# Second layer: where the splits of the operands and one sum stand in the queues

## The chip, the cores and the metric

The kernel runs on one core of a Trainium2 chip. The metric is the time of the whole program on the device in microseconds (us). The engines are named as in the profile: PE (TensorE, matrix products), ACT (ScalarE), DVE (VectorE), POOL (GpSimd), SP (SyncE, which issues all DMAs here). Each works through its own queue in order; semaphores hold an instruction until what it needs is done.

## What is computed

Attention with a decay, then two feed-forward layers on 2304 tokens of width 512. The change lies in the second layer alone:

```python
def _moe2_ref(x, w_gate, w_val, w_out):
    g = x @ w_gate                          # 512 -> 1536
    silu = g * (1.0 / (1.0 + np.exp(-g)))
    val = x @ w_val
    return (silu * val @ w_out).astype(np.float32)   # 1536 -> 512
```

## The kernel before

**Seven products.** Both matrix multiplications of the second layer are done by blocks with seven products instead of eight. Sums and differences of blocks of the weights are made ahead and stored in DRAM; those of the activations are made on the fly. The order of the products is `PO = (1, 6, 2, 7, 5, 4, 3)`; the text calls them P0 to P6 in this order. The results come together in three PSUM tiles a, b and c: P0 goes to a and ACT copies it out as p (p1 in the code); P1 to b, and DVE drains u2 = b + p1; P2 is added to a, P3 to b, and DVE drains u3 = b + p1; P4 goes to c, P5 to b, P6 to c, each drained by DVE. A product that adds to a tile has to wait until the drain before it has read this tile: P2 for the copy of p, P3 for u2, P5 for u3.

**Splits.** Each operand of a product is fp32 cut into a high and a low part, and three partial products are summed. `split_c(i, src)` (L668) makes both: a cast on ACT (L672), then the difference by DVE, or by POOL for the products 2 and 5 (`LOWP`), shown as line L116. There is one buffer `c{i}` for each product, so the split for the next round can only run when the product has read the old one.

**Input half (`in2`, L769).** Two stages of weight columns, in each three passes over the tokens (768 tokens at a time), in each pass three groups q of seven products of 12 matmuls (L783). The four outputs of a group go through silu (L762: a sigmoid on ACT, two products on DVE for one block and on POOL for three) and are stored to DRAM as g. In the last group of a pass the splits for the next pass are made; `late` (L869) puts the split of P(k-1) behind Pk and, behind P6, also the split of P6 itself. In the middle group the four sums of x (`x_sums`, L680) for the next pass are made on DVE, one behind each of P0 to P3. SP reads the x of the pass after that (`x_read`) ahead of the first group.

**Output half (`out2`, L832).** Nine items of 128 columns of tokens (each of two row halves), `NIT = 9`. An item is seven products of 18 matmuls (L842) of the stored g (tiles `gt`, read by `g_load`) with weights that stay in SBUF. During item t the four sums of g for item t+1 are made (`g_sums`, L813, into the tiles `gs` and one `gt`), one behind each of P0 to P3: the first and the fourth on POOL, the second and the third on DVE (`SUMP = (0, 3)`); and the splits for item t+1 (`g_split`), by the same `late`. The sums and splits for item 0 are made in the last pass of the input half.

All instructions of the second layer keep, engine by engine, the order in which the code issues them (`in_order`, L539). So the place of a call in `after(i)`, which runs behind each product, is the place in the queues.

Of the kernel before, what the change touches and what calls it, by code (L numbers as in the profile page):

```python
# [9 lines left out]
F32 = mybir.dt.float32  # L10
# [38 lines left out]
NPASS, NQ, NST = 3, 6, 2  # L49
NIT = NPASS * CH // 128  # L50
TCL = 84
PO = (1, 6, 2, 7, 5, 4, 3)
LOWP = (2, 5)
SUMP = (0, 3)
POS_IN = {1: 0, 2: 1, 5: 2, 6: 3, 7: 4, 3: 5, 4: 6}
POS_OUT = {2: 0, 3: 1, 5: 2, 6: 3, 7: 4, 4: 5, 1: 6}
ORD1 = "0c152cw64cowwc"
# [41 lines left out]
def body(ctx: ExitStack, tc: tile.TileContext, qk, v, f, w_in, w_out, w_gate, w_val, w_out2, mask_c, ident_c, sel_c, out):  # L99
# [547 lines left out]
    free = []  # L647
    cp = [None]
    X, xid, cmb, wu = {}, {}, {}, {}
    jobs = []  # L650

    def slot_tile(shape, dtype, name):
        s = free.pop(0)
        t = wpools[0 if s < SA else 1].tile(shape, dtype, tag=f"w{s}", name=f"{name}{s}")
        return s, t
# [4 lines left out]
    def x_read(b, p):  # L660
        SP.dma_start(out=X[b], in_=x2[2 * p + b % 2][:, b // 2 * 2:b // 2 * 2 + 2])

    def u_read(u, i):
        s, t = slot_tile([128, 2, 2, 256], F32R, "wu")
        wu[u, i] = s, t
        SP.dma_start(out=t.bitcast(F32), in_=w_u[u][(POS_IN if u < NQ else POS_OUT)[i]])

    def split_c(i, src):  # L668
        n = src.shape[1]
        c = cp[0].tile([128, 2, 2 * CH], F32R, tag=f"c{i}", name=f"c{i}")  # L670
        c = cmb[i] = c.rearrange("p h (k t) -> p h k t", k=n)
        ACT.copy(out=c[:, 0], in_=src)  # L672
        subtract(POOL if i in LOWP else DVE, c[:, 1], src, c[:, 0])

    def tt(o, a, b, op, e=None):
        (e or DVE).tensor_tensor(out=o, in0=a, in1=b, op=op)  # L676
# [3 lines left out]
    def x_sums(e=None):  # L680
        return [lambda: tt(X[5], X[1], X[0], sub, e), lambda: tt(X[4], X[3], X[5], sub, e),
                lambda: tt(X[1], X[3], X[1], sub, e), lambda: tt(X[6], X[2], X[4], sub, e)]
# [79 lines left out]
    def silu(e, C, g, p, q, blk):  # L762
# [4 lines left out]
        SP.dma_start(out=g_d[p][blk, :, :, q], in_=g[:, blk].rearrange("p (m t) -> p m t", m=NPASS))  # L767

    def in2(p, q, after):  # L769

        at, bt = (ps.tile([128, 2, 512], F32, tag=t, name=t) for t in "ab")
        ct = ps.tile([128, 2, 512], F32, tag="c", name="c")
        a, b, c = (t[:, :, :CH] for t in (at, bt, ct))
        acc = {1: (a, 1, 0), 2: (a, 0, 1), 6: (b, 1, 0), 7: (b, 0, 0), 4: (b, 0, 1), 5: (c, 1, 0), 3: (c, 0, 1)}
        p1, u2, u3 = (wk.tile([128, 2, CH], F32, tag="u", name=n, bufs=6) for n in ("p1", "u2", "u3"))
        g = wk.tile([128, 4, CH], F32, tag="g", name="g", bufs=2)
        for i in PO:
            o, s, e = acc[i]
            for mem in range(2):
                n = 0  # L780
                for x, y in ((0, 0), (1, 0), (0, 1)):
                    for kt in range(2):
                        PE.matmul(o[:, mem], lhsT=wu[q, i][1][:, mem, x, 128 * kt:128 * kt + 128], rhs=cmb[i][:, y, kt],  # L783
                                  start=bool(s and n == 0), stop=(n == 5), skip_group_check=True)
                        n += 1
            if i == 1:
                ACT.copy(out=p1, in_=a)  # L787
            elif i == 6:
                tt(u2, b, p1, add)
            elif i == 2:  # L790
                silu(DVE, a, g, p, q, 0)
            elif i == 7:
                tt(u3, b, p1, add)
            elif i == 5:
                tt(u3, c, u3, add)
                silu(POOL, u3, g, p, q, 3)
            elif i == 4:
                tt(p1, b, p1, add)
                silu(POOL, p1, g, p, q, 2)
            else:  # L800
                tt(u2, c, u2, add)
                silu(POOL, u2, g, p, q, 1)
            after(i)

    GT = {}
    sums = {}

    def g_load(t):
        GT[t] = [slot_tile([128, NQ, 128], F32, "gt") for _ in range(4)]
        for e in range(4):  # L810
            SP.dma_start(out=GT[t][e][1], in_=g_d[t // NPASS][e, :, t % NPASS])

    def g_sums(t, k):  # L813
        g = [x[1] for x in GT[t]]
        s1, s2, s4 = (sums[e][1] for e in range(3))
        tt(*((s1, g[1], g[3], add), (g[1], g[0], g[1], sub), (s2, g[3], g[1], sub), (s4, g[2], s2, sub))[k], e=POOL if k in SUMP else DVE)

    def g_split(t, i):
        g = [x[1] for x in GT[t]]
        s1, s2, s4 = (sums[e][1] for e in range(3))  # L820
        split_c(i, {1: g[0], 6: s2, 2: g[2], 7: g[1], 5: s1, 4: g[3], 3: s4}[i])
        if i == 3:
            free.extend(x[0] for x in GT.pop(t))

    def rows(t, par):
        s0 = 128 * t
        for a, b in ((s0, min(s0 + 128, S)), (max(s0, S), s0 + 128)):
            if a < b:
                d = 2 * (a // S) + par
                yield a - s0, b - s0, d * S + a % S  # L830

    def out2(t, after):  # L832
        a, b, c = (ps.tile([128, 2, 512], F32, tag=n, name=n)[:, 0, :256] for n in "abc")
        acc = {1: (a, 1), 2: (a, 0), 6: (b, 1), 7: (b, 0), 4: (b, 0), 5: (c, 1), 3: (c, 0)}
# [30 lines left out]
    def fill(n=0):  # L865
        while jobs and len(free) > n:
            u_read(*jobs.pop(0))

    def late(fn, i):  # L869

        k = PO.index(i)
        if k:
            fn(PO[k - 1])
        if k == 6:
            fn(i)

    NQS = NQ // NST
    for st in range(NST):
        for p in range(NPASS):
            final = st == NST - 1 and p == NPASS - 1  # L880
            nxt = None if final else (p + 1) % NPASS
            for q in range(NQS * st, NQS * st + NQS):
                k = q - NQS * st

                def after(i):
                    if p == NPASS - 1:
                        free.append(wu.pop((q, i))[0])
                        fill()
                    if k == 1 and i in PO[:4]:
                        if final:  # L890
                            g_sums(0, PO.index(i))
                        else:
                            x_sums()[PO.index(i)]()
                    if k == NQS - 1:
                        late((lambda i: g_split(0, i)) if final else x_split, i)

                if k == 0 and not final:
                    for e in range(4):
                        x_read(e, nxt)
                in2(p, q, after)  # L900
                if k == 0 and p == 0 and st == 0:
                    jobs += [(u, i) for u in range(4, NQ) for i in PO]
            if st == NST - 1 and p == NPASS - 2:
                free.extend(xid.values())
                g_load(0)
                for e in range(3):
                    sums[e] = slot_tile([128, NQ, 128], F32, "gs")
                g_load(1)
                jobs += [(u, i) for i in PO for u in range(NQ, 9)]
                fill()  # L910
    fill()
    assert not jobs and len(free) == 4, (jobs, free)
    for t in range(NIT):
        if t + 2 < NIT:
            g_load(t + 2)

        def after(i):
            if t + 1 < NIT:
                if i in PO[:4]:
                    g_sums(t + 1, PO.index(i))  # L920
                late(lambda i: g_split(t + 1, i), i)

        out2(t, after)
    in_order(first)
# [57 lines left out]
```

## Time and profile before

| | |
|---|---|
| median of 3 runs (lowest, highest) | 1005.52 us (1004.41, 1006.17) |
| profiled execution, its own time | 1004.43 us |
| its span, first to last instruction | 1002.6 us |
| busy: PE, DVE, ACT, POOL | 982.5, 690.1, 505.6, 538.2 us |
| mean granted clock of PE | 0.994 |
| first matmul of the input half | 586.1 us |
| first matmul of the output half | 854.9 us |

PE is busy for 98% of the span; the other engines have room on average, but not in each stretch. The granted clock is given as a share of the full 2.4 GHz. Times in rows are counted from the first instruction of the span.

### The profile page before, as it was taken

Reading aid. Unit: us, or ns where it says so; the run is one execution under the profiler, and the core shown is the slowest. Engines: PE = TensorE matmul, PEld = TensorE weight load, DVE = VectorE, ACT = ScalarE, POOL = GpSimd, SP = SyncE. Lnnn points to the kernel's source line nnn. Section 1 sums busy time; section 2 is a strip of 40 time slices with the busy share of each in tenths; the row PEclk is TensorE's granted clock in tenths of the full one; section 3 lists DMA queues with packets and bytes.
Section 4 is the critical chain, followed back from the end, with each engine's and each line's share of the span. In section 5 each row is a group of like instructions: output and inputs, shape, how many; then the busy total and the mean of one; then the engine's idle time right before and its main releaser. Section 6 shows DMA issues by size and latency. Waiting matters only on the chain. (4 is left out here: it accounts for less than half of the span.)

```text
span 1002.6 us, 18483 instructions
## 1 busy us (share of the span) xinstructions
PE 982.5 (98%) x6728; PEld 938.5 (94%) x6728; DVE 690.1 (69%) x1302; ACT 505.6 (50%) x1112; POOL 538.2 (54%) x476
## 2 busy tenths in 40 slices
PE   8999999999999999999999999999999999899998
PEld 5787877899999999999999999999999999799998
DVE  5888887687788778777775546666666565566763
ACT  6888888355545555556555422332413232344431
POOL 3555654343248677687682014645645565846642
PEclk9999999999999999999999999999999999899999
DMA  5666564433457868778767772317732339643321
GB/s 198 191 184 216 185 205 151 141 102 124 160 178 232 250 216 269 242 224 260 231 206 256 253 270 63 111 51 265 262 117 69 107 120 404 242 158 133 121 106 42
DMA packets 108555, 183.36 MB, mean 183 GB/s; under 512 B 8720, under 2 KB 71984, under 8 KB 108464
## 3 DMA queue, kind: packets, MB, share of 16 engines
q1 hardware_dynamic: 108464, 182.18, 55.2%
q8 instruction: 53, 0.87, 0.4%
q14 instruction: 38, 0.31, 0.1%
HBM read 119.15 MB, written 63.00 MB: 182 GB/s over the span
## 5 line engine op out<-in xcount | busy, mean ns | idle before, releaser
L254 PE MATMUL h<-xh,w 128*128 128x384 f32 x768 | 149.5, 335 | 0.0
L613 PE MATMUL t<-gh,w 128*128 128x384 f32 x704 | 136.6, 335 | 1.8 <-ACT gh L598 1.8
L254 PEld LDWEIGHTS h<-xh,w 128*128 128x128 f32 x768 | 134.4, 188 | 0.5 <-issue 0.5
L613 PEld LDWEIGHTS t<-gh,w 128*128 128x128 f32 x704 | 123.1, 188 | 2.6 <-ACT gh L598 2.3
L783 PE MATMUL b<-c,wu 128*128 128x384 f32 x648 | 121.7, 335 | 3.5 <-DVE u L676 3.5
L590 ACT ACTIVATE n<-h 128x384 int32<-128x384 f32 x96 | 47.1, 491 | 143.7 <-PE h L254 132.4
L592 DVE SCALAR_TENSOR_TENSOR r<-h,n 128x384 f32<-128x384 f32 x96 | 53.4, 556 | 95.0 <-ACT n L590 94.6
L783 PEld LDWEIGHTS b<-c,wu 128*128 128x128 f32 x648 | 112.8, 188 | 5.2 <-DVE u L676 5.1
L765 POOL TENSOR_TENSOR s<-u,s 128x384 f32<-128x384 f32 x36 | 44.2, 1229 | 113.1 <-ACT s L764 101.5
L408 ACT ACTIVATE P<-P,mx 128x576 f32<-128x576 f32 (+4 forms) x160 | 87.5, 547 | 4.0 <-DVE mx L401 4.0
L676 DVE TENSOR_TENSOR u<-b,p 128x768 f32<-128x768 f32 (+1 forms) x54 | 41.8, 775 | 59.7 <-PE b L783 42.2
L254 PE MATMUL h<-xl,w 128*128 128x384 f32 x384 | 82.0, 334 | 0.0
L783 PE MATMUL a<-c,wu 128*128 128x384 f32 x432 | 81.4, 336 | 0.2
L783 PE MATMUL c<-c,wu 128*128 128x384 f32 x432 | 80.7, 334 | 0.0
L401 DVE CUSTOM_DVE_ANT_0 P<-s,mask 128x576 f32<-128x576 f32 (+4 forms) x160 | 68.1, 482 | 14.0 <-PE s L377 14.0
L783 PEld LDWEIGHTS a<-c,wu 128*128 128x128 f32 x432 | 75.2, 188 | 1.8 <-ACT p L787 1.8
L116 POOL TENSOR_TENSOR w<-ta,w 128x512 fp32r<-128x512 f32 x32 | 44.6, 1395 | 59.4 <-ACT w L191 32.0
L783 PEld LDWEIGHTS c<-c,wu 128*128 128x128 f32 x432 | 75.4, 188 | 0.0
L613 PE MATMUL t<-gl,w 128*128 128x384 f32 x352 | 75.2, 334 | 0.0
L842 PE MATMUL b<-wu,c 128*128 128x256 f32 x486 | 65.4, 290 | 5.0 <-DVE u L676 5.0
L764 ACT ACTIVATE s<-u 128x384 f32<-128x384 f32 x36 | 18.9, 524 | 98.8 <-DVE u L676 98.8
L254 PEld LDWEIGHTS h<-xl,w 128*128 128x128 f32 x384 | 67.9, 188 | 0.0
(116 smaller groups left out, 2198.8 us busy)
## 6 DMA issues: line engine op xcount, KB each, us to landing
wu<-wu SPq DMA_DIRECT2D x63, 512.0 KB
wraw<-in_w_out_dram SPq DMA_DIRECT2D x28, 512.0 KB
wu<-hi SPq DMA_DIRECT2D x54, 256.0 KB
gd<-g SPq DMA_DIRECT2D x72, 192.0 KB
gt<-gd SPq DMA_DIRECT2D x36, 384.0 KB
raw<-in_qk_dram SPq DMA_DIRECT2D x16, 576.0 KB
wu<-sums SPq DMA_DIRECT2D x36, 256.0 KB
xb<-x SPq DMA_DIRECT2D x24, 384.0 KB
```

The source lines that it names most:

```text
L116: eng.tensor_tensor(out=o, in0=a, in1=b.bitcast(F32), op=ALU.subtract)
L254: PE.matmul(ps, lhsT=w[:, a, 128 * kk:128 * kk + 128], rhs=b[:, kk], start=(n == 0), stop=(n == 3 * KD - 1))
L401: DVE.tensor_tensor_reduce(out=view(P[p][:rows, c0:c0 + ext], t), in0=ss[p % 2][:rows, SAT[t][0], SAT[t][1]], in1=view(mask[:rows, m1 - ex ...
L408: ACT.activation(out=o, in_=o, func=AF.Exp, scale=-1.0, bias=mxt[p % 8][:rows, t:t + 1], accum_out=smt[p // 2 % 3][:rows, p % 2, t:t + 1])
L590: ACT.activation(out=n, in_=h, func=AF.Copy, scale=INV2PI, bias=0.25)
L592: DVE.scalar_tensor_tensor(out=r, in0=h, scalar=INV2PI, in1=n, op0=ALU.mult, op1=ALU.subtract)
L613: PE.matmul(acc[m][:, :CH], lhsT=wo[:, q, 128 * m:128 * m + 128], rhs=x, start=(j == a and n == 0), stop=False)
L676: (e or DVE).tensor_tensor(out=o, in0=a, in1=b, op=op)
L764: ACT.activation(out=s, in_=C[:, 0], func=AF.Sigmoid)
L765: e.tensor_tensor(out=s, in0=C[:, 0], in1=s, op=ALU.mult)
L783: PE.matmul(o[:, mem], lhsT=wu[q, i][1][:, mem, x, 128 * kt:128 * kt + 128], rhs=cmb[i][:, y, kt], start=bool(s and n == 0), stop=(n == 5) ...
L842: PE.matmul(ot, lhsT=cmb[i][:, x, q], rhs=wu[NQ + q // 2, i][1][:, q % 2, y], start=bool(s and n == 0), stop=(n == 3 * NQ - 1), skip_group ...
```

## The change

`late` becomes a queue of one entry that lives on across groups and items: behind a product it issues the split that waits in it and takes up the split of the product just issued. So the split of P6 is now issued behind P0 of the next group or item; the other six stay where they were. The sums of x and of g move one product further on, and the first sum of g goes from POOL to DVE (`SUMP = (3,)`). For the items, the sums 0 and 1 stand behind P1, sum 2 behind P2, sum 3 behind P3. The reads of x, the first reads of g and the reads of g two items ahead are issued behind P1 of the next group or item instead of ahead of its P0.

```diff
-SUMP = (0, 3)
+SUMP = (3,)
...
-    def late(fn, i):
-
-        k = PO.index(i)
-        if k:
-            fn(PO[k - 1])
-        if k == 6:
-            fn(i)
+    pend = []
+
+    def late(fn=None, i=None):
+
+        if pend:
+            f, k = pend.pop(0)
+            f(k)
+        if fn:
+            pend.append((fn, i))
...
-                    if k == 1 and i in PO[:4]:
+                    if final and k == 0 and i == PO[1]:
+                        free.extend(xid.values())
+                        g_load(0)
+                        for e in range(3):
+                            sums[e] = slot_tile([128, NQ, 128], F32, "gs")
+                        g_load(1)
+                        jobs.extend((u, i) for i in PO for u in range(NQ, 9))
+                        fill()
+                    if k == 1 and i in PO[1:5]:
                         if final:
-                            g_sums(0, PO.index(i))
+                            g_sums(0, PO.index(i) - 1)
                         else:
-                            x_sums()[PO.index(i)]()
+                            x_sums()[PO.index(i) - 1]()
                     if k == NQS - 1:
                         late((lambda i: g_split(0, i)) if final else x_split, i)
-
-                if k == 0 and not final:
-                    for e in range(4):
-                        x_read(e, nxt)
+                    else:
+                        late()
+
+                    if k == 0 and not final and i == PO[1]:
+                        for e in range(4):
+                            x_read(e, nxt)
+
...
     for t in range(NIT):
-        if t + 2 < NIT:
-            g_load(t + 2)
 
         def after(i):
+            k = PO.index(i)
             if t + 1 < NIT:
-                if i in PO[:4]:
-                    g_sums(t + 1, PO.index(i))
-                late(lambda i: g_split(t + 1, i), i)
+                for n in ((), (0, 1), (2,), (3,), (), (), ())[k]:
+                    g_sums(t + 1, n)
+                late(lambda i, t=t: g_split(t + 1, i), i)
+            else:
+                late()
+            if k == 1 and t + 2 < NIT:
+                g_load(t + 2)
```

The queue of ACT at the end of the first pass, before. The casts to `c_7792` and `c_7795` are the splits of P5 and P6 for the next pass, `p_7805` is the copy of P0 of the next pass:

```order
L764 ACTIVATE s<-u_7664 128x384
L672 CAST c_7792<-xb_6943 128x768
L672 CAST c_7795<-xb_6864 128x768
L787 COPY p_7805<-a 128x768
L764 ACTIVATE s<-a 128x384
```

The same place now:

```order
L764 ACTIVATE s<-u_7664 128x384
L672 CAST c_7792<-xb_6943 128x768
L787 COPY p_7798<-a 128x768
L672 CAST c_7815<-xb_6864 128x768
L764 ACTIVATE s<-a 128x384
```

The copy and the cast for P6 have changed places.

The queue of DVE at the same place, before (`u_7806` is the drain u2 of the next pass's first group):

```order
L676 TENSOR_TENSOR u_7664<-c,u_7664 128x768
L116 TENSOR_TENSOR c_7792<-xb_6943,c_7792 128x768
L116 TENSOR_TENSOR c_7795<-xb_6864,c_7795 128x768
L676 TENSOR_TENSOR u_7806<-b,p_7805 128x768
L765 TENSOR_TENSOR s<-a,s 128x384
```

And now:

```order
L676 TENSOR_TENSOR u_7664<-c,u_7664 128x768
L116 TENSOR_TENSOR c_7792<-xb_6943,c_7792 128x768
L116 TENSOR_TENSOR c_7815<-xb_6864,c_7815 128x768
L676 TENSOR_TENSOR u_7799<-b,p_7798 128x768
L765 TENSOR_TENSOR s<-a,s 128x384
```

The order of DVE is the same there: the subtraction for P6 stands ahead of u2 in both.

The queue of DVE in item 1 of the output half, before, from its drain u2 (`u_9976`) to its drain u3 (`u_9977`); `gt` and `gs` are the sums for item 2, L116 the splits for it:

```order
L116 TENSOR_TENSOR c_9961<-gs_9362,c_9961 128x768
L676 TENSOR_TENSOR u_9976<-b,p_9975 128x256
L676 TENSOR_TENSOR gt_9790<-gt_9789,gt_9790 128x768
L116 TENSOR_TENSOR c_10019<-gt_9789,c_10019 128x768
L676 TENSOR_TENSOR gs_9361<-gt_9792,gt_9790 128x768
L116 TENSOR_TENSOR c_10042<-gs_9361,c_10042 128x768
L676 TENSOR_TENSOR u_9977<-b,p_9975 128x256
```

And now (u2 is `u_9965`, u3 `u_9966`):

```order
L116 TENSOR_TENSOR c_9987<-gs_9395,c_9987 128x768
L676 TENSOR_TENSOR u_9965<-b,p_9964 128x256
L676 TENSOR_TENSOR gs_9393<-gt_9840,gt_9842 128x768
L676 TENSOR_TENSOR gt_9840<-gt_9839,gt_9840 128x768
L116 TENSOR_TENSOR c_10011<-gt_9839,c_10011 128x768
L676 TENSOR_TENSOR gs_9394<-gt_9842,gt_9840 128x768
L116 TENSOR_TENSOR c_10042<-gs_9394,c_10042 128x768
L676 TENSOR_TENSOR u_9966<-b,p_9964 128x256
```

The first sum (`gs_9393`), on POOL before, stands between u2 and the second sum.

## Rows read from the trace of the kernel before

**Rows 1.** Waits of PE over the span: waiter <- awaited: us in total, times, longest

```profile
PE b L842 <- DVE u L676: 5.0, 2, 4.7
PE b L783 <- DVE u L676: 3.5, 5, 0.7
```

**Rows 2.** Timeline, first pass boundary: start us, us, engine, line, operation [idle before <-releaser]

```profile
629.86 2.24 PE L783 MATMUL a<-c,wu 128*128 128x384 f32 x12
...
631.94 2.24 PE L783 MATMUL b<-c,wu 128*128 128x384 f32 x12
...
632.78 3.60 DVE L116 TENSOR_TENSOR c<-xb,c 128x768 fp32r<-128x768 f32 x2 [1.66 <-ACT c L672]
633.01 2.55 POOL L116 TENSOR_TENSOR c<-xb,c 128x768 fp32r<-128x768 f32 x1
633.39 0.79 ACT L787 COPY p<-a 128x768 f32<-128x768 f32 x1
...
634.23 2.38 PE L783 MATMUL a<-c,wu 128*128 128x384 f32 x12
...
636.30 0.94 DVE L676 TENSOR_TENSOR u<-b,p 128x768 f32<-128x768 f32 x1
...
637.30 2.38 PE L783 MATMUL b<-c,wu 128*128 128x384 f32 x12 [0.69 <-DVE u L676]
```

**Rows 3.** Timeline, item 0 of the output half

```profile
860.56 1.72 POOL L765 TENSOR_TENSOR s<-u,s 128x384 f32<-128x384 f32 x1
861.34 0.41 DVE L676 TENSOR_TENSOR u<-b,p 128x256 f32<-128x256 f32 x1
...
862.36 1.01 POOL L766 TENSOR_TENSOR g<-u,s 128x384 f32<-128x384 f32 x1
863.33 1.84 POOL L676 TENSOR_TENSOR gs<-gt,gt 128x768 f32<-128x768 f32 x1
...
864.06 2.32 PE L842 MATMUL c<-wu,c 128*128 128x256 f32 x18
...
865.20 0.96 DVE L676 TENSOR_TENSOR gt<-gt,gt 128x768 f32<-128x768 f32 x1 [3.45 <-POOL gs L676]
...
871.03 4.21 PE L842 MATMUL b<-wu,c 128*128 128x256 f32 x18 [4.65 <-DVE u L676]
```

**Rows 4.** Stretch 868 to 870: us, busy PE PEld DVE ACT POOL, PEclk, DMA

```profile
868.00:870.00 2.00, 0.00 (x0) 0.00 (x0) 1.15 (x1) 2.00 (x3) 1.97 (x2) 0.59 0.96 315
```

**Rows 5.** Timeline, item 2 of the output half, and P5 of item 7

```profile
892.01 1.85 POOL L676 TENSOR_TENSOR gs<-gt,gt 128x768 f32<-128x768 f32 x1
...
894.86 0.37 ACT L846 COPY p<-a 128x256 f32<-128x256 f32 x1 [1.26 <-PE a L842]
...
897.09 0.42 DVE L676 TENSOR_TENSOR u<-b,p 128x256 f32<-128x256 f32 x1 [1.55 <-PE b L842]
897.43 0.95 DVE L676 TENSOR_TENSOR gt<-gt,gt 128x768 f32<-128x768 f32 x1
898.30 0.95 DVE L116 TENSOR_TENSOR c<-gt,c 128x768 fp32r<-128x768 f32 x1
...
900.21 0.83 ACT L672 CAST c<-gs 128x768 fp32r<-128x768 f32 x1 [0.66 <-DVE gs L676]
900.25 1.86 POOL L676 TENSOR_TENSOR gs<-gt,gs 128x768 f32<-128x768 f32 x1 [6.40 <-ACT g L850]
...
901.08 1.86 DVE L116 TENSOR_TENSOR c<-gs,c 128x768 fp32r<-128x768 f32 x1 [0.95 <-ACT c L672]
901.14 2.32 PE L842 MATMUL c<-wu,c 128*128 128x256 f32 x18
...
902.86 0.41 DVE L676 TENSOR_TENSOR u<-b,p 128x256 f32<-128x256 f32 x1
...
903.32 2.42 PE L842 MATMUL b<-wu,c 128*128 128x256 f32 x18
...
979.48 2.42 PE L842 MATMUL b<-wu,c 128*128 128x256 f32 x18
```

More of the change, by code (lines that the diff above doesn't have):

```diff
@@ L902, in body @@
                     jobs += [(u, i) for u in range(4, NQ) for i in PO]
[L903 to L910, printed above, removed]
     fill()
-    assert not jobs and len(free) == 4, (jobs, free)
+    assert not jobs
     for t in range(NIT):
-        if t + 2 < NIT:
-            g_load(t + 2)
         def after(i):
+            k = PO.index(i)
             if t + 1 < NIT:
-                if i in PO[:4]:
-                    g_sums(t + 1, PO.index(i))
-                late(lambda i: g_split(t + 1, i), i)
+                for n in ((), (0, 1), (2,), (3,), (), (), ())[k]:
[5 more added lines that the diff above has]
+                g_load(t + 2)
         out2(t, after)
```

## The prediction

> **What bounds the kernel now.** I read the page's busy shares first: the matrix engine (PE) is busy 98% of 1002.6 us, so a change that touches no matmul can only win back what PE stands still or runs slowly in the second layer. The list of waits gives that: PE waits there for VectorE (DVE) alone, 5.0 us in two places of the output half and 3.5 us in five places of the input half [rows 1]. Then I read the stretches around these places in order of time.
>
> Products are called P0 to P6 in the order of issue (1, 6, 2, 7, 5, 4, 3); "split k" is the cast on ACT and the subtraction that make the operand of Pk for the next pass or item. P3 may not start before the drain u2 = b + p1 has read PSUM tile b after P1, and P5 not before the drain u3 has read it after P3. Both drains are on DVE, behind whatever stands ahead of them in its queue.
>
> At a pass boundary [rows 2] products follow each other by 2.08 us (629.86 to 631.94). P2 is due at 634.02 and starts at 634.23, after ACT's copy of p; P3 is due at 636.10 and starts at 637.30, 0.06 us after u2 has ended (636.30 + 0.94). So 1.20 us are lost, five times. DVE came late to u2 because two subtractions took 3.60 us from 632.78 on: POOL's own subtraction ran from 633.01 to 635.56, and the second one on DVE ended only 0.82 us after that.
>
> In the output half the largest stop is in item 0 [rows 3]: P4 starts at 864.06, takes 2.32 and ends at 866.38; P5 starts at 871.03. DVE spent this time on the sums for item 1, and the second of them (865.20) had to wait for the first, which is POOL's (863.33 + 1.84 = 865.17); POOL was late because it still had silu to do. In this stop the granted clock fell: 0.59 on average from 868 to 870 us [rows 4], which with levels 1 and 0.5 (2.4 and 1.2 GHz) puts the fall at 868.36, 2.0 us after PE had stopped. P5 then took 4.21 us [rows 3] where the same product takes 2.42 in item 2 [rows 5]: 1.79 us more.
>
> Item 2 stands for items 1 to 7 [rows 5]. P5 starts at 903.32, 2.18 us after P4 (901.14), and from item 2 to item 7 it comes every 15.23 us (903.32 to 979.48, five items), 2.18 for each of seven products: PE runs evenly, P5 is not held. But u3 ends at 902.86 + 0.41 = 903.27, 0.05 us ahead of it. DVE's queue from u2 to u3 fills the time between P1 and P5 with nothing to spare.
>
> **The change, part by part.** *Split 6 one product later, at five pass boundaries.* On ACT the copy of p now stands ahead of the last cast; it can start where the cast did, one cast (0.83, [rows 5]) earlier, so P2 is no longer held: 0.21 us. But on DVE the last subtraction still stands ahead of u2, since it is issued after P0 and u2 after P1. Its cast now ends about 0.8 us later, near 634.3, while the subtraction could not start before POOL's had ended at 635.56. So u2 ends at 637.24 as before, P3 starts at 637.30, and what P2 wins P3 waits. I take 0 for the five boundaries. Bounds: 0.2 us less each if the earlier copy helps after all, 0.2 us more each if the later cast does hold the subtraction; 1.0 us either way. The reads of x move behind P1 of the next group, but in SP's queue they stand behind the same stores as before, so they cost nothing; the sums of x stand one product later behind u2 instead of ahead of it, in a group where PE waits for nothing. Without that cover a sum ahead of u3 would cost what it takes, 0.95.
>
> *The first sum of the next item's activations, from POOL to DVE.* It stands between u2 and the second sum. Neighbours there start 0.87 us apart (897.43 to 898.30, [rows 5]), and POOL is idle until the third sum is done, so the new one takes 0.87 us and pushes everything behind it: the third sum, the cast that waits for it (900.21), POOL's fourth sum (900.25), the subtraction beside it (901.08, 1.86 long) and u3. P5 then starts at 903.32 + 0.87 and is that much late in items 1 to 7: 7 x 0.87 = 6.09 us. On POOL nothing on the path is won: its sum ran at 892.01 for 1.85 us, to 893.86, and DVE came to the second sum only at 897.43. Bounds: 0 if the queue turns out to have room that these rows hide, 7 x 0.95 = 6.7 if the sum costs its whole duration.
>
> *Split 6 across items.* Its cast now follows the copy of p (894.86 + 0.37 = 895.23) and takes 0.83, the subtraction 0.95: it ends near 897.05, and u2 starts at 897.09. It just fits; if it did not, u2 and so P5 would come up to 0.2 us later in each item (1.4 us in all). I take 0. The loads two items ahead keep their place in SP's queue, behind the stores of the item before.
>
> *Item 0* [rows 3]. u2 starts at 861.34 as before. The first sum comes up on DVE 0.34 us later (as the second does now, [rows 5]), while POOL has silu from 860.56 to 862.28 and the second half of it from 862.36. Where the two engines met, one waited for the other: the silu at 860.56 took 1.72 and the one at 862.36, with DVE idle, 1.01. So I let them take turns: first sum to 862.28 + 0.83 = 863.11, POOL's second half to 863.96, second sum to 864.79. From the end of the second sum to P5 it is 903.32 - 898.38 = 4.94 us in item 2. P5 at 869.73 instead of 871.03: 1.30 us won. Bounds: 2.6 if the sums meet no silu (863.50 + 4.94 = 868.44), 1.0 if the first sum waits for both halves (863.37 + 0.83 + 0.87 + 4.94 = 870.01). The stop is still 869.73 - 866.38 = 3.35 us, longer than the 2.0 after which the clock fell, so I leave the 1.79 us where they are; bounds: all of it won, or as much again lost if the clock comes back later.
>
> *The sums of item 0 itself,* in the last pass: POOL's one (1.85) now stands between two silu steps and delays two stores of g and the weight loads behind them in SP's queue by up to 2 us. POOL's next work after them comes later than that, and the products that need these weights come over 10 us later. 0.
>
> *Sum:* 0 + 6.09 - 1.30 = 4.79 us. The profiled execution took 1004.43 us (1002.6 and 1.8 around it), so 1009.22; it lies 1.09 below the median of the runs (1005.52). On the median's scale: 1005.52 + 4.79 = 1010.3 us.
>
> **The rivals.** *The forecast (0.60):* VectorE's queue in the output half becomes the bound: 1010.3; with the low bound of item 0 and of the boundaries 6.09 - 2.6 - 1.0 = 2.5, so 1008.0, with the high ones 6.7 - 1.0 + 1.0 = 6.7, so 1012.2.
>
> *The clock holds in item 0 (0.12).* The stop shrinks from 4.65 to 3.35 us; if the clock stays up, 1.79 us are won: 1008.5. For it speaks the shorter stop and that after the short stops at the pass boundaries P3 ran at full speed (2.38 us, [rows 2]); against it that the fall came after 2.0 us.
>
> *The boundaries are cured (0.10).* If u2 no longer waits behind the last subtraction there, 5 x 1.20 = 6.0 us go: 1004.3. For it: the last split does leave the tail of the pass. Against it: DVE's order, in which that subtraction still stands ahead of u2.
>
> *The sum leaves the slow engine and the path gets shorter (0.13), faster than before.* The subtraction at 901.08 takes 1.86 beside POOL and 0.95 alone (the length of the one at 898.30). If POOL, with one sum less, takes its fourth sum and its own subtraction at times that leave this one free, the queue loses 0.91 and gains 0.87: nothing is lost in items 1 to 7, item 0 wins 1.30 + 0.91, and its stop of about 2.4 us may spare the clock: 1005.5 - 0.3 - 2.2 - 1.8 = 1001.2. It decides from the point where POOL's fourth sum does not start with the end of the third; the rows show it starting 0.04 us beside the cast (900.21 and 900.25), so I hold it unlikely. The Trainium skill (GPSIMD Engine Reference, 4.1 Engine selection) says to put elementwise work on VectorE, as GpSimd needs about twice the time for operations with two inputs. The trace agrees (1.85 against 0.95), and by that rule alone eight moved sums would win 8 x 0.9 = 7.2 us; it leaves out which of the two queues PE waits for.
>
> *More than the sum is late (0.05):* if the moved split also holds u2, or the clock falls in some of the seven new stops of about 0.9 us, 1.8 us each: 1013 and above.
>
> **How the numbers follow.** A measurement of this kernel can tell about 0.2%, 2.0 us, from no change. Slower by more: the forecast but for its edge, most of the clock's case and the last one, 0.70. Within: the cured boundaries, the rest of the clock's case and that edge, 0.15. Faster: the shorter path and a part of the cured boundaries, 0.15. The likeliest case's own range is 1008.0 to 1012.2; to leave out no more than 2 in 10 it has to reach down to the cured boundaries: 1004.2 to 1012.2.
>
> **What would show it.** In the profile after: PE's waits for u in the output half nine times instead of two, each of items 1 to 7 with about 0.9 us before P5, and an item every 16.1 us; on DVE two sums back to back behind u2; in item 0 P5 about 1.3 us earlier against its P3, with a clock below 1; at the pass boundaries P2 on time and P3 late by 1.2 us as before. The prediction is wrong if items still come every 15.2 us, or if PE's wait for u is gone from the input half.

## The result, and the profile after

| | before | changed |
|---|---|---|
| median | 1006.01 us (6 runs) | 1011.13 us (6 runs) |
| ratio to before | | 1.0054, 95% interval 1.0039 to 1.0069 |
| profiled execution, its own time | 1004.43 us | 1011.03 us |
| span | 1002.6 us | 1009.2 us |

The change makes the kernel 0.54% slower, 5.1 us by the medians, where 4.8 were forecast (1010.3 us). The two profiled executions differ by 6.6 us. Of these, 1.8 lie ahead of the second layer, where no instruction has moved: its first matmul starts at 586.1 us before and at 587.9 now. From there to the end it is 416.5 and 421.3 us, 4.8 more. The starts of the matmuls in the timelines divide this further:

| us | before | changed |
|---|---|---|
| input half, first matmul to first matmul of item 0 | 268.77 | 268.90 |
| item 0, P0 to P0 of item 1 | 22.38 | 20.70 |
| items 1 to 7, each | 15.24 | 16.15 |

The waits of PE for the drains u (waiter <- awaited: us in total, times, longest), against [rows 1]:

```profile
PE b L842 <- DVE u L676: 9.0, 9, 3.3
PE b L783 <- DVE u L676: 5.3, 5, 1.1
```

In the output half there are nine waits instead of two, as forecast; the longest is shorter (3.3 against 4.7). In the input half there are five as before, and longer.

The first pass boundary, against [rows 2] (start us, us, engine, line, operation, idle before):

```profile
633.71 2.24 PE L783 MATMUL b<-c,wu 128*128 128x384 f32 x12
...
634.42 0.79 ACT L787 COPY p<-a 128x768 f32<-128x768 f32 x1
...
634.79 2.57 POOL L116 TENSOR_TENSOR c<-xb,c 128x768 fp32r<-128x768 f32 x1
635.11 0.83 ACT L672 CAST c<-xb 128x768 fp32r<-128x768 f32 x1
...
635.79 2.25 PE L783 MATMUL a<-c,wu 128*128 128x384 f32 x12
635.98 2.20 DVE L116 TENSOR_TENSOR c<-xb,c 128x768 fp32r<-128x768 f32 x1 [0.33 <-ACT c L672]
...
638.10 0.94 DVE L676 TENSOR_TENSOR u<-b,p 128x768 f32<-128x768 f32 x1
...
639.10 2.35 PE L783 MATMUL b<-c,wu 128*128 128x384 f32 x12 [1.06 <-DVE u L676]
```

P2 (635.79) now follows P1 (633.71, 2.08 earlier) on time, since the copy of p stands ahead of the last cast. But the second subtraction on DVE, whose cast ends at 635.94, starts at 635.98 and, beside POOL's (634.79 to 637.36), takes 2.20 us, so it ends 0.82 us after POOL's, as it did before; u2 follows it at 638.10, and P3 starts at 639.10, 5.39 us after P1. Before, it started 5.36 us after P1.

Item 0, against [rows 3]:

```profile
862.48 1.72 POOL L765 TENSOR_TENSOR s<-u,s 128x384 f32<-128x384 f32 x1
863.26 0.41 DVE L676 TENSOR_TENSOR u<-b,p 128x256 f32<-128x256 f32 x1
...
863.60 1.42 DVE L676 TENSOR_TENSOR gs<-gt,gt 128x768 f32<-128x768 f32 x1
...
864.28 1.61 POOL L766 TENSOR_TENSOR g<-u,s 128x384 f32<-128x384 f32 x1
865.05 1.66 DVE L676 TENSOR_TENSOR gt<-gt,gt 128x768 f32<-128x768 f32 x1
...
865.98 2.32 PE L842 MATMUL c<-wu,c 128*128 128x256 f32 x18
...
871.12 0.41 DVE L676 TENSOR_TENSOR u<-b,p 128x256 f32<-128x256 f32 x1
...
871.59 3.34 PE L842 MATMUL b<-wu,c 128*128 128x256 f32 x18 [3.29 <-DVE u L676]
...
877.49 2.32 PE L842 MATMUL a<-wu,c 128*128 128x256 f32 x18
```

The two sums follow u2 on DVE, each beside half of POOL's silu (1.42 and 1.66 us instead of 0.95). P5 starts 5.61 us after P4; it was 6.97.

The granted clock there, against [rows 4] (busy times of PE, PEld, DVE, ACT, POOL, then PEclk, DMA share, GB/s):

```profile
870.00:871.50 1.50, 0.00 (x0) 0.00 (x0) 1.50 (x2) 1.50 (x3) 1.50 (x2) 1.00 1.00 371
871.50:873.00 1.50, 1.41 (x10) 1.41 (x11) 1.41 (x3) 0.07 (x1) 1.50 (x2) 0.90 0.99 385
873.00:875.00 2.00, 2.00 (x12) 2.00 (x11) 0.74 (x2) 0.00 (x0) 2.00 (x1) 0.50 0.43 171
875.00:877.00 2.00, 2.00 (x14) 2.00 (x14) 0.39 (x1) 0.83 (x1) 0.39 (x1) 0.72 0.35 131
```

It is still full while PE stands (868.30 to 871.59), and falls about 1.1 us after PE has started again: with levels 1 and 0.5, a mean of 0.90 over 871.5 to 873 puts the fall at 872.7. By 877 it is back. From P5 to P0 of item 1 (871.59 to 877.49) it is 5.90 us; in item 2 (905.37 to 909.78, next rows) it is 4.41.

Item 2, against [rows 5]:

```profile
893.64 2.32 PE L842 MATMUL a<-wu,c 128*128 128x256 f32 x18
...
895.80 2.32 PE L842 MATMUL b<-wu,c 128*128 128x256 f32 x18
...
898.16 0.42 DVE L676 TENSOR_TENSOR u<-b,p 128x256 f32<-128x256 f32 x1
898.50 0.95 DVE L676 TENSOR_TENSOR gs<-gt,gt 128x768 f32<-128x768 f32 x1
899.48 0.96 DVE L676 TENSOR_TENSOR gt<-gt,gt 128x768 f32<-128x768 f32 x1
...
900.36 0.95 DVE L116 TENSOR_TENSOR c<-gt,c 128x768 fp32r<-128x768 f32 x1
...
902.28 2.32 PE L842 MATMUL c<-wu,c 128*128 128x256 f32 x18
902.31 1.85 POOL L676 TENSOR_TENSOR gs<-gt,gs 128x768 f32<-128x768 f32 x1 [9.26 <-issue]
...
903.14 1.85 DVE L116 TENSOR_TENSOR c<-gs,c 128x768 fp32r<-128x768 f32 x1 [0.96 <-ACT c L672]
...
904.91 0.41 DVE L676 TENSOR_TENSOR u<-b,p 128x256 f32<-128x256 f32 x1
...
905.37 2.41 PE L842 MATMUL b<-wu,c 128*128 128x256 f32 x18 [0.78 <-DVE u L676]
...
909.78 2.32 PE L842 MATMUL a<-wu,c 128*128 128x256 f32 x18
```

Two sums now stand between u2 (898.16) and the split at 900.36. From u2 to u3 it is 6.75 us, before 5.77: 0.98 more. P5 starts 3.09 us after P4, before 2.18, and the item takes 16.14 us from P0 to P0 (893.64 to 909.78).

### The profile page after: what moved, and what is told of

Same layout as the page of the kernel before. It is cut to its first block, busy times and chain, and to the rows that moved or that the text cites. A ratio compares the mean times of both kernels' runs of the same rounds, so it can differ in the third digit from the quotient of the medians.

```text
span 1009.2 us, 18462 instructions
## 1 busy us (share of the span) xinstructions
PE 982.4 (97%) x6728; PEld 939.2 (93%) x6728; DVE 694.0 (69%) x1311; ACT 505.0 (50%) x1112; POOL 518.2 (51%) x467
## 5 line engine op out<-in xcount | busy, mean ns | idle before, releaser
L765 POOL TENSOR_TENSOR s<-u,s 128x384 f32<-128x384 f32 x36 | 40.8, 1134 | 123.7 <-ACT s L764 122.1
L116 POOL TENSOR_TENSOR w<-ta,w 128x512 fp32r<-128x512 f32 x32 | 44.9, 1403 | 60.0 <-ACT w L191 32.8
L842 PEld LDWEIGHTS b<-wu,c 128*128 128x128 f32 x486 | 60.9, 194 | 10.8 <-DVE u L676 10.8
```

The costliest lines, as they stand in the source:

```text
L116: eng.tensor_tensor(out=o, in0=a, in1=b.bitcast(F32), op=ALU.subtract)
L765: e.tensor_tensor(out=s, in0=C[:, 0], in1=s, op=ALU.mult)
L842: PE.matmul(ot, lhsT=cmb[i][:, x, q], rhs=wu[NQ + q // 2, i][1][:, q % 2, y], start=bool(s and n == 0), stop=(n == 3 * NQ - 1), skip_group ...
```

## The experiments

Every kernel was timed beside the kernel before on the same chip; the ratios are to it, with their 95% intervals in brackets. Times of single steps are from the one profiled execution of each run. "Behind Pk" is the place in the queues where an operation is issued.

**1. The first sum on DVE in its old place.** Edit of the kernel before:

```diff
-SUMP = (0, 3)
+SUMP = (3,)
```

> The kernel before with one edit: the first sum of g on DVE instead of POOL, in its old place behind P0, so on DVE ahead of u2. Theory (what costs is the place between u2 and u3): DVE is idle there for about 1.5 us in items 1 to 7, so items keep 15.2 us; in item 0 P5 comes about 1.3 us earlier, with a longer wait at P3 (about 2.2 us instead of 0.5) and a shorter one at P5. 1003.0 to 1005.5 us. Rival 1 (DVE has too much work wherever the sum stands): items 16.1 us, about 1011. Rival 2 (the moved splits cost, not the sum): 1004.5, as the theory, so this run tells theory and rival 1 apart.

Measured: 1003.48 us, ratio 0.9977 (0.9963 to 0.9992). Items 2 to 7 take 15.24 us, item 1 15.53, item 0 19.23 (22.38 before). DVE's rows in an item:

```profile
892.57 0.95 DVE L676 TENSOR_TENSOR gs<-gt,gt 128x768 f32<-128x768 f32 x1
...
894.89 0.42 DVE L676 TENSOR_TENSOR u<-b,p 128x256 f32<-128x256 f32 x1 [1.36 <-PE b L842]
```

The sum (892.57) fills a gap in which DVE would wait for P1, 1.36 us are still left of it at 894.89, and u2 is not late. So the same operation on the same engine costs 0.9 us an item in one place and nothing in another. In item 0 P2 to P3 took 4.30 us, 2.14 too long, and P4 to P5 3.95, 1.8 too long; PE stood for 1.98 and 1.63 us there, and the granted clock stayed at 1.00 in both stops. Rival 1 is out.

**2. The first sum back on POOL, splits and places as changed.**

```diff
-SUMP = (3,)
+SUMP = (0, 3)
```

> The changed kernel with one edit: the first sum of g back on POOL; splits and places as changed. Theory: items return from 16.1 to 15.2 us, P5 of item 0 waits about 4.6 us again, 1006 us as the kernel before. Rival 1 (work on DVE): 1006 too. Rival 2 (split of P6 behind P0, or the sums one product later, hold u2): items stay at 16.1 us, 1011.

Measured: 1005.30 us, ratio 0.9991 (0.9977 to 1.0005). Items take 15.16 us, P4 to P5 of item 0 6.97 as before. The moved split costs nothing; rival 2 is out. It even wins 0.08 us an item. In item 0 the same stop of 4.65 us as before shows another fall of the clock (columns as above):

```profile
872.06 3.92 PE L842 MATMUL b<-wu,c 128*128 128x256 f32 x18 [4.65 <-DVE u L676]
...
870.00:872.00 2.00, 0.00 (x0) 0.00 (x0) 2.00 (x2) 2.00 (x3) 2.00 (x2) 1.00 0.95 341
872.00:874.00 2.00, 1.94 (x10) 1.95 (x11) 1.91 (x3) 0.04 (x1) 2.00 (x2) 0.58 0.35 139
```

The clock is full until 872 here, and 0.58 over the next 2 us puts the fall at 872.3: 4.9 us after PE had stopped (867.41) and 0.3 after it had started again. Before, the fall came 2.0 us after PE had stopped. From P5 to P0 of item 1 it is 5.91 us, 1.56 more than in item 2 of this run.

**3. The first sum on DVE behind P0, with the moved split.** Edit of the changed kernel:

```diff
-                for n in ((), (0, 1), (2,), (3,), (), (), ())[k]:
+                for n in ((0,), (1,), (2,), (3,), (), (), ())[k]:
```

> The changed kernel with one edit: in the items the sums stand behind P0, P1, P2, P3 again, the first still on DVE, so ahead of u2 and of the last split's subtraction. Theory: items 15.2 us, item 0 as in the first run, 1003.0 to 1005.5 us. Rival 1: 1011. Rival 2: 1011, if it is the split of P6 behind P0 that costs.

Measured: 1003.54 us, ratio 0.9977 (0.9964 to 0.9991); items 15.16 us. (Of an item's four sums the change had moved only the first, from behind P0 to behind P1.) In item 0 both the sum and the last split's subtraction stand ahead of u2 here: PE stands for 2.95 us, P2 to P3 takes 5.26, more than in the first run, and the clock fell (0.86 over 864 to 866, 0.50 over the next 2 us).

**4. At the pass boundaries the split of P6 behind P1.** Edit of the changed kernel (the block that frees the tiles of x moves behind it):

```diff
-                    else:
+                    elif k or i != PO[0]:
                         late()
```

> The changed kernel with one edit: at the pass boundaries of the input half the split of P6 is issued behind P1 of the next group, so on DVE behind u2; the items stay as changed. Theory (P3 waits at the boundary because that subtraction stands ahead of u2): the five waits of about 1.1 us before P3 go, 6.0 us less than the changed kernel, 1005. Rival (POOL's subtraction or the silu holds u2, or the wait comes back at P5): the input half stays at 268.9 us, 1011.

Measured: 1004.57 us, ratio 0.9984 (0.9969 to 0.9999): 6.6 us less than the changed kernel's median. The first boundary:

```profile
637.03 2.24 PE L783 MATMUL a<-c,wu 128*128 128x384 f32 x12
637.33 0.96 DVE L676 TENSOR_TENSOR u<-b,p 128x768 f32<-128x768 f32 x1 [0.45 <-PE b L783]
638.20 1.20 DVE L116 TENSOR_TENSOR c<-xb,c 128x768 fp32r<-128x768 f32 x1
...
639.11 2.24 PE L783 MATMUL b<-c,wu 128*128 128x384 f32 x12
```

u2 (637.33) stands ahead of the subtraction (638.20), and P3 starts 2.08 us after P2. The input half takes 262.15 us, 6.75 less, and PE does not wait in it at all; the items stay at 16.16. So the five waits hang on that one place in DVE's queue.

**5. u3 freed in the items.** Edit of the fourth run's kernel; `lag` is the number of splits that wait:

```diff
-        if pend:
+        if len(pend) >= lag:
...
-                for n in ((), (0, 1), (2,), (3,), (), (), ())[k]:
+                for n in ((), (0, 1), (), (2,), (3,), (), ())[k]:
                     g_sums(t + 1, n)
-                late(lambda i, t=t: g_split(t + 1, i), i)
+                late(lambda i, t=t: g_split(t + 1, i), i, 2 if t or k else 9)
-            else:
+            elif pend:
```

> The fourth run's kernel with, in the items, every split one product further on (split of P6 behind P1, so behind u2; split of P1 behind u3) and the second pair of sums behind P3 and P4: on DVE only the sums 0 and 1 and two splits are left between u2 and u3, and none of them waits for a cast that waits for a sum; the first sum stays on DVE. Theory (PE waits only for u2 and u3, wherever they stand behind other work): input half 262.2 us, item 0 15.2 to 16.2 us with the clock up, items 1 to 7 15.2 us: 6.6 + 6.5 + 0.5 us less than before, 991.5 to 993.5. Rival (the work on DVE comes due elsewhere: g at the end of an item, or a split too late for its product): items of 16 us, 998 and above.

Measured: 997.88 us, ratio 0.9927 (0.9911 to 0.9943). A miss; it went the way the rival had named, by a smaller amount: items take 15.64 us, item 0 17.61. In items 1 to 7 P3 and P5 are on time; now P6 is late:

```profile
890.28 0.95 DVE L676 TENSOR_TENSOR gs<-gt,gt 128x768 f32<-128x768 f32 x1
...
891.90 2.32 PE L842 MATMUL b<-wu,c 128*128 128x256 f32 x18
...
892.19 1.85 DVE L116 TENSOR_TENSOR c<-gs,c 128x768 fp32r<-128x768 f32 x1 [0.96 <-ACT c L672]
...
893.97 0.41 DVE L676 TENSOR_TENSOR g<-c,u 128x256 f32<-128x256 f32 x1
...
894.52 2.39 PE L842 MATMUL c<-wu,c 128*128 128x256 f32 x18 [0.30 <-DVE g L676]
```

The third sum (890.28), its cast and the subtraction beside POOL (892.19) stand ahead of P4's drain (893.97), which frees tile c for P6 (894.52). P5 to P6 takes 2.62 us instead of 2.26, and P6 to P0 2.23. The wait had moved from one drain to the next. In item 0 P5 still waits 0.40 us, and P6 waits 1.62: P4's drain ends at 863.13 there, behind a subtraction that ends at 862.79. (The profile puts this wait down to a cast that ends at the same time.)

**6. Runs 3 and 4 together.**

> The third and fourth run's edits together on the changed kernel: split of P6 behind P1 at the pass boundaries, the first sum on DVE behind P0 in the items. Theory: the two gains add, since they lie in different halves: 262.2 us in the input half, items of 15.2 us, item 0 19 to 20 us: 996 to 997.5. Rival (they share a cause, such as DVE's total work): 1003.

Measured: 995.83 us, ratio 0.9908 (0.9894 to 0.9923): input half 262.15, items 15.16, item 0 19.80 us, just under the expected 996 to 997.5. The gains add: against the changed kernel's ratio of 1.0054, runs 3 and 4 win 0.0077 and 0.0070, and both together 0.0146.

**7. The fifth run's kernel with the first sum on POOL** (`SUMP = (0, 3)`).

> The fifth run's kernel with the first sum on POOL. Theory: in items 1 to 7 nothing changes (POOL makes it long before DVE needs it), in item 0 the second sum on DVE again waits for POOL's, behind silu, and u3 comes about 2 us late: 993.5 to 996. Rival (the engine of the sum matters in every item): items differ from 15.2 us.

Measured: 998.28 us, ratio 0.9930 (0.9916 to 0.9944). Outside the expected time, since it shares the late P6 of run 5. But against that run the items are the same (15.64 to 15.65 but for one of 15.75), and item 0 takes 1.4 us more (19.02): P5 waits 1.79 us there for u3, in run 5 0.40. So in this order of the queues the engine of the sum matters in item 0 alone, as the theory has it.

**8. Run 6 with item 0 arranged anew.** Only item 0 (t = 0) differs from run 6; `pops` is the number of waiting splits that are issued:

```diff
-                for n in ((0,), (1,), (2,), (3,), (), (), ())[k]:
+                for n in (((0,), (1,), (2,), (3,), (), (), ()) if t else ((), (0, 1), (), (2,), (3,), (), ()))[k]:
                     g_sums(t + 1, n)
-                late(lambda i, t=t: g_split(t + 1, i), i)
+                late(lambda i, t=t: g_split(t + 1, i), i, 1 if t else (0, 1, 0, 0, 2, 2, 2)[k])
```

> The sixth run's kernel with item 0 alone arranged anew: its own split of P6 behind u2, the first two sums behind u2, the splits for item 1 from P4 on, the third sum behind u3, so that between u2 and u3 stand two sums and one split. Theory: item 0 takes 15.3 to 16 us instead of 19.8 and the clock stays up, the rest as in the sixth run: 4 to 4.5 us less than that, about 991.5. Rival (the backlog on DVE is only moved to item 1, whose P3 or P5 waits instead): no change, 996.

Measured: 994.39 us, ratio 0.9876 (0.9857 to 0.9895), the fastest of all. Item 0 takes 15.11 us, seven products and no stop. But item 1 takes 17.52:

```profile
867.92 2.27 DVE L116 TENSOR_TENSOR c<-gt,c 128x768 fp32r<-128x768 f32 x1
...
871.31 0.94 DVE L676 TENSOR_TENSOR gs<-gt,gt 128x768 f32<-128x768 f32 x1
872.18 0.94 DVE L116 TENSOR_TENSOR c<-gs,c 128x768 fp32r<-128x768 f32 x1
...
873.04 0.41 DVE L676 TENSOR_TENSOR u<-b,p 128x256 f32<-128x256 f32 x1
...
873.51 2.41 PE L842 MATMUL b<-wu,c 128*128 128x256 f32 x18 [0.73 <-DVE u L676]
...
879.25 2.42 PE L842 MATMUL b<-wu,c 128*128 128x256 f32 x18 [1.17 <-DVE u L676]
```

DVE comes to u2 of item 1 (873.04) with the splits that item 0 put off still ahead of it, and P3 waits until 873.51; P5 then waits another 1.17 us for u3 (879.25). Item 0 takes 4.69 us less than in run 6, item 1 2.36 more than there: half of the gain came due, and the rival was half right.

**9. The fourth sum on DVE too** (`SUMP = ()` in the changed kernel).

> The changed kernel with the fourth sum on DVE as well (behind P3, so behind u3); POOL has no sum left. Tests what the subtraction of the second split costs beside POOL. If it takes 1.85 us only because POOL's fourth sum holds it, it takes about 0.95 here, u3 comes 0.9 us earlier, items go from 16.15 to 15.25 us and the time to about 1005, with one more operation on DVE. Rival 1 (DVE's total work costs): items of 17 us, 1018. Rival 2 (POOL's own subtraction, next in its queue, holds it as long): items stay at 16.1 us, 1011.

Measured: 1006.60 us, ratio 1.0003 (0.9991 to 1.0014); items 15.69 us but for one of 15.96, where 15.25 were expected. An item:

```profile
902.28 0.96 DVE L116 TENSOR_TENSOR c<-gs,c 128x768 fp32r<-128x768 f32 x1 [0.95 <-ACT c L672]
...
903.49 2.28 DVE L676 TENSOR_TENSOR gs<-gt,gs 128x768 f32<-128x768 f32 x1
...
903.63 2.41 PE L842 MATMUL b<-wu,c 128*128 128x256 f32 x18
...
905.69 0.41 DVE L676 TENSOR_TENSOR g<-c,u 128x256 f32<-128x256 f32 x1
...
906.25 2.39 PE L842 MATMUL c<-wu,c 128*128 128x256 f32 x18 [0.21 <-DVE g L676]
```

The subtraction at 902.28 takes 0.96 us where it took 1.85 (903.14 in the changed kernel), and P4 to P5 is 2.20 again: the long subtraction was POOL's doing. But the fourth sum itself takes 2.28 beside POOL's subtraction, P4's drain (905.69) comes behind it, and P6 starts late: P5 to P6 takes 2.62 us. Half the gain is given back. The mechanism of the prediction's rival with the shorter path exists, then, but the change did not bring it about, since POOL's fourth sum still starts with the end of the third.

## Why the prediction was right

- **Items 1 to 7** (forecast 7 x 0.87 = 6.09 us): measured 7 x 0.91 = 6.4. The mechanism was right, the term 5% small. The new sum costs more than the distance of its neighbours: the second sum starts 0.98 us after it (898.50 to 899.48), not 0.87. The second one overwrites a tile that the first one reads; whether that is why, no run tests. Part of it came back, as u2 starts 2.36 us after P1 instead of 2.43. Runs 1 and 3 show that it is the place, run 2 that it is the sum and not the split. The engine alone (run 1) and the place alone (run 2) cost nothing; it takes both.
- **Item 0** (forecast 1.30 us won): P4 to P5 shrank by 1.36. DVE and POOL took turns as was worked out from the lengths in [rows 3]: counted from the start of P3 (861.81 before, 863.73 now, 1.92 later), the two sums were forecast to end at 865.03 and 866.71, and they end at 865.02 and 866.71.
- **The clock** (forecast: it falls and costs 1.79 as before): it fell and cost 5.90 - 4.41 = 1.49; from P5 to P0 before it was 6.23, 1.81 more than in item 2 there. The step behind it was weak: it took the 2.0 us after which the clock fell before for a measure of the stop, while now it fell 4.4 us after PE had stopped, when PE was running again. Run 2 has the very stop of before, 4.65 us, and there the fall came after 4.9 us and cost 1.56. So the 0.3 us by which the clock cost less now are not shown to come from the shorter stop, and that this term came out is in part luck. Why the clock falls when it does these runs don't settle.
- **The pass boundaries** (forecast 0): the input half takes 0.13 us more. P2 is on time and P3 late, as forecast. That the later cast would leave the subtraction where it was came out to 0.1 us; run 4 shows what the order of DVE was worth: 6.62 us less than before (268.77 to 262.15), not 5 x 1.20, since P4 too came 0.13 us late behind each stop.
- **The split of P6 across items** (forecast 0, just fitting): 0.08 us an item are won (run 2). So PE did not run quite evenly in the items before, as the prediction read it from the mean of 2.18: P4 to P5 took 2.18, P5 to P6 2.26, the others 2.16.
- **The chances.** Of the rivals only the shorter path had something to it (run 9). Adding the sum of 4.79 to the median of the first three runs, 1005.52, gave 1010.3; on the median of all six it would be 1010.8.

## What to carry to other kernels

Before an operation is moved to a faster engine, look at what stands behind it in that engine's queue: here 0.95 us of work on DVE cost 0.9 us an item between two drains that PE waits for, and nothing a few instructions earlier, in a gap. When a split or a copy is put off, ask whether it now stands behind or still ahead of the next drain; one place further was worth 6.75 us in the input half. And when one drain is freed, look at once at the next: in runs 5, 8 and 9 a drain behind the moved work was late.

## What the runs showed of the hardware

- DVE and POOL hold each other up when both combine tiles in SBUF: the same subtraction on DVE takes 0.95 us beside an idle POOL, 1.85 behind POOL's sum (903.14) and 2.20 where it meets POOL's own subtraction (635.98); POOL's silu product takes 1.61 beside DVE (864.28) and 1.01 alone [rows 3]; the drains, which read PSUM, kept their 0.41 (863.26, 904.91). This let the times of item 0 be worked out to 0.1 us.
- In item 0 the granted clock fell behind a stop of PE of 4.65 us before (2.0 us after PE had stopped, while it stood) and of 4.65 in run 2 (4.9 us after, when it ran again), of 3.3 in the changed kernel (4.4 us after) and of 2.4 in run 9; behind the stops of 2.0 and 1.6 us in run 1 and of 1.8 in run 7 it stayed at 1.00. The same stop was followed by the fall at two different times, and it cost 1.5 to 1.8 us each time where it was measured here.
- The part of the program ahead of the second layer, the same in all, ended between 585.7 and 589.1 us in these profiles. A difference of a few us in the end of two profiled executions says nothing before it is taken stage by stage.
